# The first expert slot's rows gathered into the query load buffers, and the third value chunk joined to the first two in every second unit

## The chip, the cores and the metric

One core of a Trainium2 chip runs the program. The metric is device time in microseconds (us) of one execution. A measurement of this kernel can tell about 0.2% (2 us) from no change.

## The reference, cut to what matters

Attention comes first: 8 batches, 12 heads, 448 tokens, head size 64, with a root-mean-square norm on queries and keys. Its result is the input of a mixture of 8 experts, where each token goes to the one expert with the largest gate value.

```python
q_n, k_n = rmsnorm(q, g_q), rmsnorm(k, g_k)
scores = scale * q_n @ k_n.T
attn = exp(scores - max(scores)); attn /= sum(attn)
x = (attn @ v)                          # 3584 tokens x 768
logits = x @ w_gate + modality_bias[modality_id]
e_idx = argmax(logits)                  # one expert for each token
out[e_idx == e] = gate_w * relu(x @ w1[e]) @ w2[e]
```

## The kernel before

**Attention.** A unit is two heads of one batch, and there are 48 (NU). A unit takes 7 steps (NJ), one for each 128 of its 896 keys; step n belongs to unit i = n // 7 and has j = n % 7. In a step TensorE (PE) makes the scores of the unit itself, transposed (`st`, line 1019, two matmuls, four at j = 3), and scores of a unit two ahead for its maxima (`sa`, lines 986 and 991). ScalarE (ACT) takes the exponential of `st`; VectorE (DVE) takes the maximum of `sa`. Each of the two kinds has two PSUM buffers (`ps_s`, `ps_a`), so `st` waits for the exponential of the `st` two before it, and `sa` for the maximum of the `sa` two before it. Between these PE places, by the table PLAN, the transposes of queries and keys (`tr`, line 910), of maxima (`mt`), the value products (`av`), the sums and gate products (`sm`, lines 1083 and 1090) and the transposes of the result (`xt`, line 1127).

The value products of unit u run in the steps of unit u + 1. They come in four chunks: chunks 0 and 1 at j = 1, chunk 2 at j = 4, chunk 3 at j = 6 (`av` in PLAN is (1, 1, 4, 6)). A chunk 0 to 2 is two matmuls of 64 columns, one for each head, which the trace shows as four records. Chunk 3 holds the tail of one head and the head of the other; its weights are put together by `values(u)`, two copies of 64x64, at j = 2 of unit u + 1. `xt` of a unit runs six units later at j = 4, behind `av` and, in every fourth unit (i = 4m + 1), behind four gate products.

POOL (GpSimd) adds up the exponentials, norms queries and keys (`norm`, 26 steps ahead of its unit) and issues the indirect transfers (gathers and weights). SP issues all other transfers from one queue in order: among them the moves of queries and keys between partitions (line 923), which PE's `sa` and `st` read.

**Experts.** The tokens are worked through in slots of 256 tokens. For slot 0 the rows of x are gathered by two indirect transfers into `xrw` (`xgather`), written to a DRAM buffer (`xkeep`, line 557), read back in another layout (`xfetch`, line 563), transposed by DVE in three groups (`xturn`), and split into two parts by ACT and DVE; the first product (`mm1_half`, line 609) reads them. `xrw` holds normed queries and keys until the last unit has been transposed. `r1[0]` is the load buffer of the queries, of six units, and takes the first expert's weights (`wload`) afterwards.

Every engine's instructions run in the order in which they are written here, each engine with its own queue. A line number 52 or 53 is a recording helper's; there the tile names tell which instruction it is.

Of the kernel before, what the change touches and what calls it, by code (L numbers as in the profile page):

```python
# [19 lines left out]
NT, DM, DFF, NE = 3584, 768, 1024, 8  # L20
CP, NCH = 112, 4
NJ = 7
NP = H // 2
NU = B * NP
# [42 lines left out]
def kernel(  # L67
# [15 lines left out]
    V, A, G = (Deferred(e, n) for e, n in ((nc.vector, "op"), (nc.scalar, "act"), (nc.gpsimd, "dma")))  # L83
# [338 lines left out]
    r1 = [bp.tile([128, 3 * DFF], F32, name=f"r1_{i}") for i in range(2)]  # L422
    xrw = bp.tile([128, 4 * DM], F32, name="xrw")
# [12 lines left out]
    def view(t, off, p, *dims):  # L436
        n = 1
        for d in dims:
            n *= d
        a = t[:p, off : off + n]  # L440
        if len(dims) > 1:
            ax = " ".join("abcd"[: len(dims)])
            a = a.rearrange(f"p ({ax}) -> p {ax}", **dict(zip("abcd"[1:], dims[1:])))
        return a
# [27 lines left out]
    vd_b = [view(at_l, 8 * DM - 128 * (i + 1), 128, 128) for i in range(2)]  # L472
# [40 lines left out]
    def wload(s, which, halves=(0, 1), pairs=(0, 1)):  # L513
        tb, i = tb_of(s)
        for h in halves:
            if which == 0:
                G.indirect_dma_start(out=r1[h], out_offset=None, in_=w1v,
                                     in_offset=IOFF(ap=tb["wi"][:, i, h : h + 1], axis=0),
                                     bounds_check=NE * 256 - 1, oob_is_err=False)
                continue  # L520
            for c in pairs:
                G.indirect_dma_start(out=r2[h][:, 2 * DM * c : 2 * DM * (c + 1)], out_offset=None, in_=w2v,
                                     in_offset=IOFF(ap=tb["vi"][:, i, 2 * h + c : 2 * h + c + 1], axis=0),
                                     bounds_check=NE * DFF // 2 - 1, oob_is_err=False)
# [21 lines left out]
        return view(xrw, 0, 128, 8, DM // 4)  # L546

    def xs_(s):
        return view(xrw, 0 if s < 2 else 2 * DM, 128, 2, DM)

    def xgather(s, t):
        src = x_d[:NT1] if s < NS1 else x_d[:]
        G.indirect_dma_start(out=xs_(s)[:, t], out_offset=None, in_=src,
                             in_offset=IOFF(ap=entry(s, t)[:, 0:1].bitcast(I32), axis=0))

    def xkeep(s):
        SY.dma_start(xg_d[s].rearrange("(t p) d -> p t d", t=2), xs_(s))

    def xfetch(s):
        if s not in (0, 2):  # L560
            xkeep(s)
        for g in range(4):
            SY.dma_start(xv(s)[32 * g : 32 * g + 32],
                         xg_d[s][:, DM // 4 * g : DM // 4 * (g + 1)].rearrange("(b p) d -> p b d", p=32))
# [244 lines left out]
    if True:  # L809
# [8 lines left out]
        HB = {}  # L818
# [244 lines left out]

        def values(u):
            for h, r in enumerate((LO, HI)):
                A.copy(vd_b[u % 2][r, 64 * h : 64 * h + 64], HB[u // 3]["v"][r, u % 3, 3])

        def avcopy(u):
            t = T[u]
# [305 lines left out]
        def put(n, *what):  # L1375
            plan.setdefault(n, []).append(what)

        P = PLAN
        AVJ, XTJ, XTE, SMJ, LAJ, RCJ = (P[x] for x in ("av", "xt", "xte", "sm", "la", "rc"))
# [7 lines left out]
        def xt_at(u):  # L1387
            if u < NU - 8:
                return NJ * (u + 6) + XTJ
            return NJ * (NU - 2 + (u - NU + 8) // 2) + XTE[u % 2]  # L1390

        def when(what, u):
            return P["first"].get((what, u), NJ * u - P[what])

        for u in range(NU):
            for j in range(NJ):
                jj = ((0, 1, 2, 4, 5, 6, 3) if u < P["early"] else (3, 0, 1, 2, 4, 5, 6))[j]
                put(when("sa", u) + j * (P["sastep"] if u == 0 else 1), "sa", u, jj)
            put(when("mt", u), "mt", u)
            if u < NU - 1:  # L1400
                for c in range(4):
                    put(NJ * (u + 1) + (AVJ[c] if u < NU - 2 else min(AVJ[c], 6)), "av", u, c)
            put(xt_at(u), "xt", u)
            if u % 2:
                put(NJ * (u + 1) + (SMJ if u < NP * (B - 2) else P["sml"]), "sums", u - 1)
            if u % 4 == 3:
                put(NJ * (u + 2) + (LAJ if u < NP * (B - 2) else min(LAJ, 4)), "gates", u // 4)
                put(NJ * (u + 2) + (RCJ if u < NP * (B - 2) else min(RCJ, 6)), "recips", u // 4)
            put(when("tk", u), "tr", u, 1)
            put(when("tq", u), "tr", u, 0)  # L1410
            put(when("nq", u), "norm", u, 0)
            put(when("nk", u), "norm", u, 1)
            put(when("sk", u), "sq", u, 1)
            put(when("sq", u), "sq", u, 0)
            if ("rs", u) in P["first"]:
                put(when("rs", u), "rs", u // 3, P["rs0"].get(u, 0), u % 3 + 1)
            elif u > 8 and u % 3 == 2:
                put(when("rs", u), "rs", u // 3, 0, 3)
            if 5 < u < 10:
                put(when("ld", u), "load", u)  # L1420
            elif u > 9 and u % 2 == 0:
                put(when("ld", u) - 1, "load", u, 2, (0,))
                put(when("ld", u) + 1, "load", u, 2, (1,))

        for n in range(P["start"], NJ * NU):
# [63 lines left out]
            if 0 <= i < NU and j in CSJ:  # L1489
                h = CSJ.index(j)  # L1490
# [20 lines left out]
            if i > 0 and j == 2:  # L1511
                values(i - 1)
            if i == NU - 1 and j == 4:
                values(i)
# [9 lines left out]
            if n == P["gc2"]:  # L1524
                table_consts()
            for t in range(2):
                if n == NJ * (NU - 3) - 2 + t:
                    xgather(0, t)
            for h in range(2):
                if n == NJ * (NU - 3) - 1 + 6 * h:  # L1530
                    wload(0, 0, (h,))
            if n == NJ * (NU - 3) + 2:
                xkeep(0)
            if n == NJ * (NU - 3) + 5:
                xfetch(0)
            if i >= NU - 2 and j in P["s1"]:
                split1(P["s1"].index(j), i - NU + 2)
# [22 lines left out]
        u, g = NU - 1, NU // 4 - 1  # L1560
# [52 lines left out]
        for s in range(NSTAT):  # L1613
# [32 lines left out]
            for b_ in range(16):  # L1646
                t, j = divmod(b_, 8)
# [100 lines left out]
```

## Time and profile before

| | |
|---|---|
| median of 3 runs | 1034.41 us (1032.71 to 1034.77) |
| profiled execution | 1034.98 us, its span 1033.3 us |
| PE busy | 1013.8 us (98%) |
| DVE, ACT, POOL busy | 743.5, 709.0, 715.9 us |
| granted clock | 0.998 of full speed |

The profile is of one execution; the span runs from its first to its last instruction, and 1.7 us lie outside. Shares of busy time are averages over the attention (to about 535 us) and the experts behind it.

### The profile page before, as it was taken

To read this page: it belongs to the slowest core of one execution; us is meant where nothing else is said; L and a number is where in the kernel's file an instruction comes from. 1 tells how busy PE (TensorE), PEld (TensorE's weight loads), DVE (VectorE), ACT (ScalarE), POOL (GpSimd) and SP (SyncE) were. 2 spreads that over 40 slices of the span, in tenths; PEclk is the share of its full clock that TensorE was granted. 3 is DMA by queue.
4 is the path that set the end of the run, shared out by engine and by line. 5 is a ranking of instruction groups with operands and counts; after the bars stand their busy time and mean duration, and the time that the engine had idled before them with its cause. 6 is when DMAs were issued, how large, how long until landed. Compare 5 with 4: busy or idle time off the path is not lost. (4 is left out here: it accounts for less than half of the span.)

```text
span 1033.3 us, 18863 instructions
## 1 busy us (share of the span) xinstructions
PE 1013.8 (98%) x6462; PEld 818.9 (79%) x6462; DVE 743.5 (72%) x1260; ACT 709.0 (69%) x1379; POOL 715.9 (69%) x747
## 2 busy tenths in 40 slices
PE   9899999999999999999989999999999999999997
PEld 7655666666666666656559999999999999999995
DVE  6777888887888788886667986755685567556740
ACT  7897999889999899888655555545554455545531
POOL 7788798989788887889856646865545554565361
PEclk9999999999999999999999999999999999999999
DMA  8776667868677786766748506144572342234162
GB/s 197 187 170 138 153 141 183 178 141 185 160 168 162 160 186 148 167 116 126 228 121 286 94 20 195 32 123 123 150 279 66 119 123 79 65 105 123 40 210 92
DMA packets 147900, 148.20 MB, mean 143 GB/s; under 512 B 72702, under 2 KB 137682, under 8 KB 147284
## 3 DMA queue, kind: packets, MB, share of 16 engines
q1 hardware_dynamic: 122398, 105.08, 43.0%
q0 software_dynamic: 25328, 41.82, 12.8%
q8 instruction: 53, 0.87, 0.4%
q14 instruction: 51, 0.42, 0.2%
q10 hardware_dynamic: 70, 0.02, 0.0%
HBM read 150.31 MB, written 33.39 MB: 178 GB/s over the span
## 5 line engine op out<-in xcount | busy, mean ns | idle before, releaser
L609 PE MATMUL ph<-xw,w1w 128*128 128x256 f32 x2016 | 246.1, 284 | 1.7 <-ACT at_w2lw L52 0.8
L609 PEld LDWEIGHTS ph<-xw,w1w 128*128 128x128 f32 x2016 | 243.9, 192 | 3.3 <-issue 1.1
L52 DVE TENSOR_REDUCE at_hlw<-sa 128x1 f32<-128x448 f32 x336 | 205.1, 619 | 26.3 <-PE sa L991 24.7
L1019 PE MATMUL st<-w1w 128*128 128x448 f32 (+1 forms) x480 | 183.5, 432 | 2.4 <-ACT at_w2lw L52 1.1
L52 POOL DMA_INDIRECT r<-in_moe_w_dram,tb_w x60 | 84.0, 1399 | 53.4 <-DVE w1w L52 38.1
L52 ACT ACTIVATE hhw<-ph 128x512 fp32r<-128x512 f32 x56 | 33.5, 597 | 121.2 <-PE ph L609 121.2
L639 PE MATMUL py<-w2lw,hhw 128*128 128x384 f32 x448 | 113.8, 335 | 0.0
L52 ACT ACTIVATE r2w<-st 128x448 f32<-128x448 f32 x168 | 91.0, 544 | 32.8 <-PE st L1019 26.6
L52 DVE TENSOR_TENSOR w1w<-r,w1w 128x768 fp32r<-128x768 f32 x112 | 103.9, 958 | 11.0 <-ACT w1w L52 9.9
L991 PE MATMUL sa<-w1w 128*128 128x448 f32 (+1 forms) x288 | 108.0, 375 | 3.6 <-DVE at_hlw L52 3.3
L52 POOL DMA_INDIRECT r2w<-in_moe_w_dram,tb_vi x48 | 50.0, 1041 | 84.7 <-DVE w2lw L52 75.7
L52 ACT CAST w1w<-xw 64x448 fp32r<-64x448 f32 x188 | 105.8, 563 | 3.7 <-issue 1.4
L52 DVE TENSOR_TENSOR w2lw<-r2w,w2ha 128x1536 fp32r<-128x1536 f32 x28 | 49.1, 1757 | 81.0 <-ACT w2ha L52 81.0
L1019 PEld LDWEIGHTS st<-w1w 128*128 128x128 f32 (+1 forms) x480 | 86.1, 190 | 25.5 <-issue 10.7
L1019 PE MATMUL st<-w1w,w2ha 65*128 65x448 f32 x288 | 100.5, 369 | 0.0
L52 POOL TENSOR_TENSOR r2w<-r2w 128x448 f32<-128x448 f32 (+1 forms) x72 | 82.9, 1152 | 24.0 <-DVE r2w L52 15.1
L52 ACT ACTIVATE at_w2lw<-st 128x448 f32<-128x448 f32 x168 | 90.6, 544 | 12.1 <-PE st L1019 6.9
L52 POOL TENSOR_TENSOR xrw<-r,at_hlw 112x512 f32<-112x512 f32 x95 | 97.6, 1047 | 0.5
L52 ACT CAST w1w<-r 128x768 fp32r<-128x768 f32 x112 | 95.3, 904 | 0.1
L52 ACT ACTIVATE yw<-py,ltn 128x384 f32<-128x384 f32 x55 | 29.3, 578 | 79.1 <-PE py L639 75.5
L639 PEld LDWEIGHTS py<-w2lw,hhw 128*128 128x128 f32 x448 | 80.9, 188 | 0.0
L52 POOL TENSOR_TENSOR r2w<-r2w,at_w2lw 64x448 f32<-64x448 f32 (+1 forms) x48 | 54.7, 1140 | 31.3 <-DVE r2w L52 15.7
(302 smaller groups left out, 2208.1 us busy)
## 6 DMA issues: line engine op xcount, KB each, us to landing
w1w<-xw SPq DMA_DIRECT2D x216, 112.0 KB
xg<-xrw SPq DMA_DIRECT2D x14, 768.0 KB
xrw<-xg SPq DMA_DIRECT2D x56, 192.0 KB
r<-in_q_dram SPq DMA_DIRECT2D x19, 448.0 KB
r<-in_k_dram SPq DMA_DIRECT2D x19, 448.0 KB
w2ha<-xw SPq DMA_DIRECT2D x72, 112.0 KB
w1w<-w1w SPq DMA_DIRECT2D x48, 112.0 KB
r2w<-in_v_dram SPq DMA_DIRECT2D x24, 224.0 KB
```

The source lines that it names most:

```text
L52: return fn(*a, **kw)
L609: PE.matmul(ps[:, i], lhsT=lt_, rhs=rt_[:, c], start=n == 0, stop=n == 17)
L639: PE.matmul(ps[n][:, :384], lhsT=lt_[:, j, 128 * t : 128 * t + 128], rhs=rt_[:, 384 * n : 384 * n + 384], start=j == 0 and m == 0, stop=j ...
L991: PE.matmul(ps[:, :S], lhsT=t["qq"][r, h, a : a + 128], rhs=t["kk"][h][r], start=True, stop=True)
L1019: PE.matmul(ps[:, :S], lhsT=l, rhs=t["qq"][:, h] if first else t["ql"][0:65, h], start=first and (j != 3 or h == 0), stop=not first and (j ...
```

## The change

Three things are changed. The third chunk (c = 2) of units u = 8, 10, ..., 40 (17 units) moves from j = 4 to j = 1, behind the first two. `values` of units 8 to 41 copies on DVE instead of ACT. The rows of slot 0 are gathered into `r1[0]` (its first three query buffers, whose last reader is `norm` of unit 44) at steps 300 and 301 instead of into `xrw` at 313 and 314; `xkeep(0)` goes from step 317 to 307 and `xfetch(0)` from 320 to 312. `xfetch` still writes `xrw`.

```diff
     def xs_(s):
-        return view(xrw, 0 if s < 2 else 2 * DM, 128, 2, DM)
+        return view(r1[0], 0, 128, 2, DM) if s == 0 else view(xrw, 0 if s < 2 else 2 * DM, 128, 2, DM)
...
         def values(u):
             for h, r in enumerate((LO, HI)):
-                A.copy(vd_b[u % 2][r, 64 * h : 64 * h + 64], HB[u // 3]["v"][r, u % 3, 3])
+                copy = V.tensor_copy if 8 <= u < 42 else A.copy
+                copy(vd_b[u % 2][r, 64 * h : 64 * h + 64], HB[u // 3]["v"][r, u % 3, 3])
...
                 for c in range(4):
-                    put(NJ * (u + 1) + (AVJ[c] if u < NU - 2 else min(AVJ[c], 6)), "av", u, c)
+                    aj = AVJ[1] if c == 2 and u % 2 == 0 and 8 <= u < 41 else AVJ[c]
+                    put(NJ * (u + 1) + (aj if u < NU - 2 else min(aj, 6)), "av", u, c)
...
-                if n == NJ * (NU - 3) - 2 + t:
+                if n == 300 + 1 * t:
                     xgather(0, t)
...
-            if n == NJ * (NU - 3) + 2:
+            if n == 307:
                 xkeep(0)
-            if n == NJ * (NU - 3) + 5:
+            if n == 312:
                 xfetch(0)
```

On PE, in unit 11 (where chunks of unit 10 run), the rows before are these; `sa_4` is the `sa` of step 4.

```order
L991 MATMUL sa_0_1817<-w1w 128x448
L1061 MATMUL av_1819<-r2w,at_w2lw 64x448 x4
L1002 MATMUL mt_1824<-idn,at_hlw 7x128
...
L991 MATMUL sa_4_1868<-w1w 128x448
L1061 MATMUL av_1819<-r2w,at_w2lw 64x448 x2
L1127 MATMUL xt_1872<-idn,at_hhw 112x128 x4
L1019 MATMUL st_5_1896<-w1w 128x448 x2
```

In the changed program the same place reads as follows.

```order
L991 MATMUL sa_0_1817<-w1w 128x448
L1061 MATMUL av_1819<-r2w,at_w2lw 64x448 x6
L1002 MATMUL mt_1826<-idn,at_hlw 7x128
...
L991 MATMUL sa_4_1870<-w1w 128x448
L1128 MATMUL xt_1872<-idn,at_hhw 112x128 x4
L1019 MATMUL st_5_1896<-w1w 128x448 x2
```

Two matmuls have moved from behind `sa_4` to the four behind `sa_0`, and `xt` now follows `sa_4` at once. On DVE the two copies stand between two maxima in the changed program, ahead of the subtraction `w1w<-tr,xw`:

```order
L52 TENSOR_REDUCE at_hlw<-sa_1_1839 128x1
L52 COPY at_w2lw<-at_w2lw 64x64 x2
L52 TENSOR_REDUCE at_hlw<-sa_2_1857 128x1
L52 TENSOR_TENSOR w1w<-tr_0_1859,xw 128x448
L52 TENSOR_REDUCE at_hlw<-sa_4_1870 128x1
```

Before, the same rows stood there without the line of the copies, which ACT had. On POOL, around step 300, the changed program has the two gathers ahead of the last `norm` (the two rows `xrw<-r`, of unit 47):

```order
L379 DMA ltn<-l_d,ta_lr 128x4
L52 DMA r_0_158<-x_d,ltn 128x768
L52 TENSOR_TENSOR r2w<-r2w 128x448
L52 TENSOR_TENSOR at_hhw<-r2w 128x448
L52 DMA r_0_158<-x_d,ltn 128x768
L52 TENSOR_TENSOR xrw<-r_0_158,at_hlw 112x2x4x64
L52 TENSOR_TENSOR xrw<-r_1_159,at_hlw 112x2x4x64
```

Before, both gathers stood ten rows further on, behind the norms and eight additions, right ahead of the first weights' transfer.

## Rows read from the trace of the kernel before

**Rows 1.** Busy time by stage: stretch, length, then each engine's busy time.

```profile
94.00:422.00 328.00, 328.00 (x1807) 208.21 (x1807) 271.82 (x530) 293.82 (x685) 276.62 (x317) 1.00 0.73 164
520.00:537.00 17.00, 14.19 (x80) 9.23 (x74) 13.45 (x18) 10.22 (x22) 7.64 (x9) 1.00 0.44 94
```

**Rows 2.** Timeline of PE in unit 27: start, length, instruction, count.

```profile
314.25 1.72 PE L1061 MATMUL av<-r2w 128*64 128x448 f32 x8
315.91 0.28 PE L1002 MATMUL mt<-idn,at_hlw 128*7 128x128 f32 x1
...
318.49 0.37 PE L991 MATMUL sa<-w1w 128*128 128x448 f32 x1
318.79 0.97 PE L1061 MATMUL av<-r2w 128*64 128x448 f32 x4
319.69 0.65 PE L1127 MATMUL xt<-idn,at_hhw 128*112 128x128 f32 x4
320.09 0.65 PE L1019 MATMUL st<-w1w 128*128 128x448 f32 x2
```

**Rows 3.** Timeline of PE in unit 46, an `xt` without value products ahead.

```profile
516.44 0.37 PE L1019 MATMUL st<-w1w,w2ha 65*128 65x448 f32 x1
516.65 0.60 PE L1127 MATMUL xt<-idn,at_hhw 128*112 128x128 f32 x4
517.00 0.64 PE L1019 MATMUL st<-w1w 128*128 128x448 f32 x2
```

**Rows 4.** Timeline of DVE and PE, end of unit 27 and start of 28.

```profile
317.87 0.62 DVE L52 TENSOR_REDUCE at_hlw<-sa 128x1 f32<-128x448 f32 x1 [0.40 <-PE sa L991]
...
318.82 0.62 DVE L52 TENSOR_TENSOR w1w<-tr,xw 128x448 fp32r<-128x448 f32 x1 [0.33 <-ACT xw L52]
...
321.60 0.61 DVE L52 TENSOR_REDUCE at_hlw<-sa 128x1 f32<-128x448 f32 x1
...
322.56 0.37 PE L986 MATMUL sa<-xw 128*128 128x448 f32 x1
```

**Rows 5.** Busy time of DVE alone, from that subtraction to that maximum's end.

```profile
318.82:322.21 3.39, 3.25 (x11) 1.00 0.75 173
```

**Rows 6.** DVE's groups of instructions from 100 to 420 us: total, mean ns.

```profile
L52 DVE SCALAR_TENSOR_TENSOR r2w<-r2w,half 128x448 f32<-128x448 f32 x16 | 12.3, 770 | 0.0
...
L52 DVE TENSOR_TENSOR at_hlw<-sp,rs 112x64 f32<-112x64 f32 x14 | 2.3, 218 | 0.2
...
L52 DVE TENSOR_TENSOR ra<-lo,ra 112x32 f32<-112x32 f32 x5 | 1.0, 196 | 0.2
```

**Rows 7.** Timeline of ACT in unit 27, the exponentials of its last two steps.

```profile
320.84 1.16 ACT L52 ACTIVATE at_w2lw<-st 128x448 f32<-128x448 f32 x2 [0.15 <-PE st L1019]
```

**Rows 8.** Timeline of the end of the attention, slot 0's rows being turned.

```profile
511.30 0.38 SPq L557 DMA_DIRECT2D xg<-xrw  x1
...
526.75 1.15 DVE L52 STREAM_TRANSPOSE r2w<-xrw 128x512 f32<-128x512 f32 x1 [2.75 <-DMA xrw<-xg]
...
527.93 0.62 ACT L52 CAST xw<-r2w 128x512 fp32r<-128x512 f32 x1 [1.36 <-DVE r2w L52]
...
530.56 0.62 ACT L52 CAST xw<-r2w 128x512 fp32r<-128x512 f32 x1 [0.61 <-DVE r2w L52]
...
529.57 0.68 PE L1019 MATMUL st<-w1w 128*128 128x448 f32 x2 [1.07 <-ACT at_w2lw L52]
```

**Rows 9.** Timeline of POOL and PE, the last norm and the gathers.

```profile
488.95 2.04 POOL L52 TENSOR_TENSOR xrw<-r,at_hlw 112x512 f32<-112x512 f32 x2
...
502.87 0.94 POOL L52 DMA_INDIRECT xrw<-x_d,ltn  x1 [0.30 <-issue]
...
493.08 0.55 PE L910 MATMUL tr<-idn,xrw 112*128 112x112 f32 x4
```

**Rows 10.** Timeline of POOL and DVE beside each other, units 26 and 27.

```profile
312.52 1.54 DVE L52 SCALAR_TENSOR_TENSOR r2w<-r2w,half 128x448 f32<-128x448 f32 x1
...
316.51 2.05 POOL L52 TENSOR_TENSOR xrw<-r,at_hlw 112x512 f32<-112x512 f32 x2
```

## Prediction

> **What bounds the kernel now.** I read the busy time by stage first. From 94 to 422 us, the body of the attention, PE is busy for all of 328.00 us, and ACT, POOL and DVE for 294, 277 and 272 [rows 1]. So in this stage whatever PE no longer has to do shortens the kernel, but only until another engine's chain becomes the later one: ACT has a tenth of the stage free, and a stall of PE can come from a local chain long before an average is full. Then I read the stretch where attention ends: of 17 us PE is busy for 14.19 [rows 1], the largest hole behind the start. The timeline of that stretch says why: DVE waits 2.75 us for the rows of slot 0 to come back from DRAM, ACT waits for DVE, and PE waits 1.07 us for ACT (three shorter waits follow) [rows 8]. Those two places are what the change touches.
>
> **The third chunk, as PE sees it.** In unit 27 the run of two chunks takes from 314.25 to 315.91, 1.66 us, and the lone chunk from 318.79 to 319.69, 0.90 us [rows 2]. A third chunk inside the run therefore costs 1.66 - 0.90 = 0.76 us. The lone chunk starts 0.30 us behind `sa`, and from `xt` behind it to the next `st` are 0.40 us: 0.30 + 0.90 + 0.40 = 1.60 us from `sa` to `st` [rows 2]. Where no value product stands ahead, `xt` starts 0.21 us behind the matmul before it and `st` 0.35 us later, 0.56 us [rows 3]. So step 4 loses 1.04 us, step 1 gains 0.76, and PE's own saving is 0.28 us. This holds for the 8 of the 17 units where `xt` follows at once (u = 10, 14, ..., 38). In the other nine (u = 8, 12, ..., 40) gate products stand between; no row shows them right behind `sa`. They start between 0.21 and 0.30 us behind it, so the saving is 0.90 - 0.76 = 0.14 at the least and 0.23 at the most. Gate products are matmuls of few columns like the value chunk, which starts after 0.30, so I take 0.14. Sum on PE alone: 8 x 0.28 + 9 x 0.14 = 3.5 us.
>
> **What the other engines let through.** Up to `sa` of step 4 ACT and DVE follow PE as before; then PE asks for their work 1.04 us sooner. In unit 27 DVE's chain from the subtraction at 318.82, which waits for ACT and so for `tr` on PE, to the maximum that ends at 321.60 + 0.61 = 322.21 is busy for 3.25 of 3.39 us: it can't move up [rows 4, 5]. The first `sa` of unit 28, at 322.56, needs that maximum's PSUM buffer. It can come 322.56 - 322.21 = 0.35 us sooner, less 0.05 for the hand-over (an estimate): 0.30 instead of 1.04. The chain is this long because six small instructions of the routing stand in it. Such a routing occurs five times from 100 to 420 us [rows 6], and by the program's order all five stand in step 4 of one of the 8 units (11, 15, 23, 27, 35). There 0.74 us are given back, 5 x 0.74 = 3.7 us. The three others have no routing; on ACT the exponential of step 5 had been idle for 0.15 us only [rows 7], but the next product needs it only behind chunk 3, and ACT also loses the two copies. I take no loss there; the bound is 3 x 0.74 = 2.2 us. In the nine units with gate products 0.90 us are asked for, and the gate products and `xt` still lie between, so no loss. Attention in all: 3.5 - 3.7, or 0.2 us slower, bounded by 3.5 faster and, with the three, 2.4 slower.
>
> **The copies.** ACT is relieved of 34 pairs. In unit 27 its exponentials wait for PE's `st` anyway, so I count nothing; the bound is in the term above. On DVE no copy of this form is in the trace. The nearest row by size is a product of 112x64 at 0.22 us [rows 6]: 0.45 for two. They land where DVE idles 0.40 us ahead of the next maximum and 0.33 ahead of the subtraction [rows 4], 0.73 in all, so they are covered. If they take longer than that, all of the rest goes into the chain above.
>
> **Slot 0.** Gathers 13 steps sooner, the store 10 and the fetch 8 steps (a step is some 1.36 us: `sa` of step 4 of unit 27 at 318.49, of step 7 at 322.56 [rows 2, 4]) bring the fetch to before 515 us, well ahead of DVE's first turn at 524.0 (526.75 less the wait). The wait of 2.75 us goes. What is late next is ACT: the first group's cast moves up by its own wait of 1.36 us only, since the exponential ahead of it is PE's pace; of the second cast's 0.61 I take half, as DVE's turns now wait for ACT's casts between them [rows 8]. 1.36 + 0.30 = 1.65 us for PE; bounds 0 (if the weights' casts alone hold PE) and 2.8 (17.00 - 14.19 [rows 1]).
>
> **What the gathers are put in front of.** On POOL a gather takes 0.94 us with 0.30 of issue ahead of it, 1.24 us [rows 9], and two now stand ahead of unit 47's norm, which ended at 488.95 + 2.04 = 490.99 us. It would end at 490.99 + 2.48 = 493.47, and the transposes that read it start at 493.08: up to 0.39 us of stall, down to 0 if POOL's idle time takes them. I take 0.35. Further on POOL is even, since the gathers are gone there. The weights of slot 0 now wait on POOL for the store to have read `r1[0]`; the store ends some 500 us by the same shift, before they are due.
>
> **The sum.** - 0.2 + 1.65 - 0.35 = 1.1 us faster. The profiled execution took 1034.98 us (span 1033.3 and 1.7 around it): it would take 1033.9. It lies 0.57 us above the median, 1034.41, for which I predict **1033.3 us**.
>
> **Rivals.**
> (a) DVE's chain gives way and all of PE's saving comes through: 3.5 + 1.65 - 0.35 = 4.8, 1029.6 us; with the whole wait at the end 1028.5. For it: PE's side is certain to 0.1 us, and 8 + 9 units repeat it. Against it: rows 4 and 5 show no gap in that chain.
> (b) Slower: the copies on DVE are held up by POOL. At 317.5 us, where they go in, POOL is in the middle of two norms of 1.02 us each, and a DVE instruction that met a POOL addition took 1.54 us against a mean of 0.77 in its group [rows 6, 10]. If each pair waits for one norm, it is 1.02 + 0.45 = 1.47 us long, 0.74 over the cover; in the five units that is 3.7 us, 1037.0. If both copies wait, 2.49 - 0.73 = 1.76, times five 8.8, 1042.1. It decides from 0.73 + 1.1 / 5, about 0.95 us for a pair. The Trainium skill speaks for this: its page SBUF — State Buffer (Who interferes with whom) says that a VectorE copy in a two-port mode and a GpSimd instruction exclude each other, the later one fully blocked. The row with 1.54 us agrees for an instruction with two inputs; no row shows it for a copy.
> (c) SP stands still. It issues in order, and the store of slot 0 now stands ahead of unit 47's moves. The second gather was issued at 502.87 and the store went out at 511.30, 8.4 us later [rows 8, 9]. Issued near 490, the gather would then hold SP to 498.7 and six moves behind it at some 0.6 us each would come at up to 502.5, for an `sa` near 504: up to 2 us, 1035.3. Against it: weights were being loaded at 504 us, and not at 490, so the gather should land in about half the time.
> That the change doesn't do what it says can be left out: the order shows both moves.
>
> **Chances.** Forecast 0.42, its own range 1031.8 to 1035.0; (a) 0.28; (b) 0.20; (c) 0.10. Faster by over 0.2% means under 1032.3: (a) and 0.08 of the forecast, 0.36. Slower means over 1036.5: 0.17 of (b) and 0.01 of the forecast, 0.18. Within: 0.33 + 0.03 + 0.10 = 0.46. The range goes from 1029.5 (the middle of (a); 0.11 is left out below) to 1037.2 (one norm; 0.08 is left out above).
>
> **What would show it.** In the new trace of units 11, 15, 23, 27, 35 PE should wait for DVE's maximum at the first `sa` of the next unit, and those pairs of units should be some 0.45 us longer; units with gate products should be 0.14 shorter. The DVE copies' length against 0.95 us decides on (b). At the end DVE's wait for the fetch should be gone and PE's holes there should come to about 1.2 us instead of 2.8. At 493 us `tr` should wait under 0.5 us for the norm. I am wrong if PE waits in units 9 to 42 come to more than 4.5 us or to less than 1.5, or if a new wait stands at unit 47.

## The result, and the profile after

The changed kernel takes 1047.09 us (median of 4 runs, 1046.81 to 1050.16) where the kernel before takes 1033.99: a ratio of 1.0133, with a 95% interval of 1.0121 to 1.0146. That is 13 us slower, where 1.1 us faster was forecast, and outside the range. The profiled execution has a span of 1045.3 us, 12.0 more than before.

Busy time by stage of the changed kernel, as [rows 1] has it for the kernel before; the end of the attention now lies 13 us later:

```profile
94.00:422.00 328.00, 319.65 (x1742) 201.89 (x1742) 299.53 (x562) 272.91 (x610) 267.84 (x305) 0.99 0.70 157
533.00:550.00 17.00, 15.27 (x86) 9.65 (x80) 14.05 (x21) 10.02 (x22) 10.14 (x10) 1.00 0.15 45
```

In the body of the attention PE, busy throughout before, has lost 8.4 us to idleness, and DVE's busy time has risen from 271.82 to 299.53. The end has improved: 15.27 of 17 us are busy instead of 14.19. So the loss is in the body, and DVE got more work there than the two short copies per unit should bring. DVE's groups of instructions from 100 to 420 us (total in us, mean in ns) say what it is:

```profile
L52 DVE TENSOR_REDUCE at_hlw<-xrw 112x8 f32<-112x512 f32 x60 | 40.5, 675 | 0.0
L52 DVE COPY at_w2lw<-at_w2lw 64x64 f32<-64x64 f32 x28 | 24.3, 869 | 0.2
L52 DVE COPY at_w2lw<-r2w 64x64 f32<-64x64 f32 x26 | 20.2, 775 | 0.2
```

A copy of 64 elements a partition takes 0.8 us in the mean, longer than a reduction of 512. The timeline of unit 26 shows why: DVE, POOL and PE where the copies for unit 25 stand (`values` runs one unit later).

```profile
310.66 3.74 DVE L52 COPY at_w2lw<-r2w 64x64 f32<-64x64 f32 x2
314.43 0.19 DVE L52 TENSOR_SCALAR rs<-sp 112x32 f32<-112x32 f32 x1
...
315.04 0.62 DVE L52 TENSOR_TENSOR lg<-sp,rs 112x64 f32<-112x64 f32 x4
...
310.03 0.96 POOL L1235 DMA_INDIRECT l_d<-ltk,posi  x1 [0.16 <-issue]
311.01 2.05 POOL L52 TENSOR_TENSOR xrw<-r,at_hlw 112x512 f32<-112x512 f32 x2
313.01 1.13 POOL L52 TENSOR_TENSOR r2w<-r2w 128x448 f32<-128x448 f32 x1
314.30 0.96 POOL L1235 DMA_INDIRECT l_d<-ltk,posi  x1 [0.17 <-issue]
...
315.81 0.88 PE L1128 MATMUL xt<-idn,at_hhw 128*112 128x128 f32 x4 [2.17 <-DVE lg L52]
```

The pair starts while POOL issues an indirect transfer, and then POOL works through three instructions that stand one behind the other, to 313.01 + 1.13 = 314.14. The first copy takes 3.54 us and ends 0.06 us behind the last of them; the second takes 0.19 us. Behind the copies DVE's small products on `sp` are late, and PE waits 2.17 us for them at `xt`. Elsewhere the same pair can be short; these rows are of units 14 (the pair starts 0.06 us into an indirect transfer of POOL) and 40 (POOL idle to 466.18):

```profile
180.47 0.38 DVE L52 COPY at_w2lw<-r2w 64x64 f32<-64x64 f32 x2
...
180.41 0.96 POOL L1235 DMA_INDIRECT l_d<-ltk,posi  x1 [0.15 <-issue]
...
465.48 0.38 DVE L52 COPY at_w2lw<-at_w2lw 64x64 f32<-64x64 f32 x2
...
466.18 0.27 POOL L53 TENSOR_TENSOR at_hlw<-at_hlw 112x48 f32<-112x48 f32 x1 [1.36 <-ACT at_hlw L53]
```

What PE waited for from 100 to 480 us (sum, times, longest):

```profile
PE sa L991 <- DVE at_hlw L52: 3.5, 10, 0.8
PE sa L986 <- DVE at_hlw L52: 3.0, 6, 0.6
PE xt L1128 <- DVE lg L52: 2.2, 1, 2.2
PE xt L1128 <- DVE at_hlw L52: 0.8, 2, 0.4
PE st L1019 <- ACT r2w L52: 0.6, 1, 0.6
```

All but 0.6 of these 10.1 us are waits for DVE. In the kernel before, PE waited in the same stretch for 0.9 us (0.5 for ACT, 0.4 for DVE).

### The profile page after: what moved, and what is told of

It is laid out like the page before. It is cut to its first block, busy times and chain, and to the rows that moved or that the text cites. A ratio compares the mean times of both kernels' runs of the same rounds, so it can differ in the third digit from the quotient of the medians.

```text
span 1045.3 us, 18868 instructions
## 1 busy us (share of the span) xinstructions
PE 1017.9 (97%) x6462; PEld 819.4 (78%) x6462; DVE 791.2 (76%) x1328; ACT 693.1 (66%) x1311; POOL 711.2 (68%) x747
## 5 line engine op out<-in xcount | busy, mean ns | idle before, releaser
L991 PE MATMUL sa<-w1w 128*128 128x448 f32 (+1 forms) x288 | 110.5, 384 | 7.1 <-DVE at_hlw L52 6.4
```

The source lines that it names most:

```text
L991: PE.matmul(ps[:, :S], lhsT=t["qq"][r, h, a : a + 128], rhs=t["kk"][h][r], start=True, stop=True)
```

## The experiments

Eleven kernels undo, isolate or rewrite parts, and one cuts the copies. To say where a difference lies, each profiled execution is cut at instructions that all programs share. Of PE's eight `st` of 65x448 in a unit, the profile names eight `st<-w1w,w2ha` in three units of four and none in the fourth, six in the mean; number 6u + 1 of these is called mark u here. It is the same instruction in every program, but only every fourth mark (8, 12, ..., 44) is the start of the unit of its number: mark 9 lies in unit 8, mark 42 in unit 41, mark 47 in unit 46. B is from mark 9 to mark 42, C on to mark 47, D from there to the end of the span, which the profile gives to 0.1 us. B, C and D are each of one execution: e2's was the fastest of its five and e11's the slowest of its seven. The part ahead of B differed by up to 2.1 us between executions, with the kernel before the longest; no edit touches it. Each ratio is against runs of the kernel before on the same chip.

| kernel | ratio (95%) | B, us | C, us | D, us |
|---|---|---|---|---|
| before | 1 | 344.35 | 50.32 | 516.86 |
| changed | 1.0133 (1.0121 to 1.0146) | 358.02 | 51.66 | 515.98 |
| e1 chunk alone | 1.0035 (1.0022 to 1.0049) | 347.95 | 50.35 | 516.73 |
| e2 copies on DVE alone | 1.0174 (1.0151 to 1.0196) | 359.99 | 51.75 | 517.01 |
| e3 slot 0 alone | 1.0003 (0.9991 to 1.0015) | 345.59 | 53.05 | 516.17 |
| e4 changed, copies as maxima | 1.0215 (1.0199 to 1.0231) | 368.74 | 51.37 | 516.00 |
| e5 changed, copies on ACT | 1.0032 (1.0013 to 1.0051) | 346.91 | 52.15 | 516.85 |
| e6 changed, copies as reductions | 1.0027 (1.0012 to 1.0041) | 347.28 | 52.98 | 516.74 |
| e7 reductions alone | 1.0018 (1.0004 to 1.0032) | 346.66 | 51.53 | 517.97 |
| e8 chunk in gate units alone | 0.9991 (0.9974 to 1.0009) | 343.98 | 50.23 | 518.41 |
| e9 as e8, and slot 0 behind the norm | 1.0007 (0.9996 to 1.0018) | 343.78 | 51.79 | 515.77 |
| e10 slot 0 behind the norm alone | 1.0011 (0.9997 to 1.0025) | 344.29 | 53.04 | 516.65 |
| e11 chunk in the other eight units | 1.0044 (1.0027 to 1.0061) | 352.85 | 50.30 | 516.58 |
| e12 changed, copies halved | 1.0279 (1.0258 to 1.0301) | 373.25 | 51.49 | 515.76 |

**e1, the chunk alone.** The kernel before with this:

```diff
-put(NJ * (u + 1) + (AVJ[c] if u < NU - 2 else min(AVJ[c], 6)), "av", u, c)
+aj = AVJ[1] if c == 2 and u % 2 == 0 and 8 <= u < 41 else AVJ[c]
+put(NJ * (u + 1) + (aj if u < NU - 2 else min(aj, 6)), "av", u, c)
```

> The kernel before with the third chunk's move alone; the copies of `values` stay on ACT. Theory L (the copies on DVE wait for POOL's instructions, and that is the loss): 1032 to 1036 us; the nine units with gate products give back some 0.17 us each (pairs of units in the changed kernel whose copies ran in 0.19 us), the others between 0.2 of gain and 0.45 of loss. Theory M (the moved chunk is the loss, since DVE's chain is then late at the next unit): 1042 us or more, with PE waiting for a maximum at the first `sa` of units 12, 16, 24, 28 and 36.

1.0035, some 3.6 us: that is 1037.6 us on the scale of the expectation, over theory L's range (up to 1036) and well short of theory M (from 1042). PE, DVE and PE again at the end of unit 27, as in [rows 2] and [rows 4]:

```profile
315.21 2.48 PE L1061 MATMUL av<-r2w 128*64 128x448 f32 x12
317.61 0.28 PE L1002 MATMUL mt<-idn,at_hlw 128*7 128x128 f32 x1
...
320.17 0.36 PE L991 MATMUL sa<-w1w 128*128 128x448 f32 x1
320.37 0.60 PE L1127 MATMUL xt<-idn,at_hhw 128*112 128x128 f32 x4
320.73 0.65 PE L1019 MATMUL st<-w1w 128*128 128x448 f32 x2
...
320.51 0.62 DVE L52 TENSOR_TENSOR w1w<-tr,xw 128x448 fp32r<-128x448 f32 x1 [0.33 <-ACT xw L52]
...
323.30 1.15 DVE L52 TENSOR_REDUCE at_hlw<-sa 128x1 f32<-128x448 f32 x2
...
323.00 0.47 PE L1019 MATMUL st<-w1w 128*128 128x448 f32 x1
323.31 0.36 PE L1019 MATMUL st<-w1w,w2ha 65*128 65x448 f32 x1
323.96 0.47 PE L986 MATMUL sa<-xw 128*128 128x448 f32 x1 [0.29 <-DVE at_hlw L52]
```

The run with the third chunk takes 317.61 - 315.21 = 2.40 us instead of 1.66, and from `sa` to `st` of step 4 PE now needs 0.56 us instead of 1.60, as worked out. But DVE's chain from the subtraction to the last maximum starts 320.51 - 320.17 = 0.34 us behind that `sa`, as before (0.33), and is as long as before (2.79 to the start of the maximum, 2.78 before), so the next unit's `sa` waits. From mark 11 to mark 13, a stretch with one moved chunk (in unit 11), it is 162.60 - 136.47 = 26.13 us here and 163.36 - 137.78 = 25.58 before: 0.55 longer.

**e2, the copies alone.** The kernel before with this:

```diff
-A.copy(vd_b[u % 2][r, 64 * h : 64 * h + 64], HB[u // 3]["v"][r, u % 3, 3])
+copy = V.tensor_copy if 8 <= u < 42 else A.copy
+copy(vd_b[u % 2][r, 64 * h : 64 * h + 64], HB[u // 3]["v"][r, u % 3, 3])
```

> The kernel before with the copies of `values` on DVE alone. Theory L: 1043 to 1048 us, the copies take 0.19 us where POOL is idle and else end some 0.05 us behind a POOL instruction, mean about 0.8. Theory M: 1034 to 1036.

1.0174, over theory L's range: the copies alone are slower than the whole change. They take 0.88 us in the mean:

```profile
L52 DVE COPY at_w2lw<-at_w2lw 64x64 f32<-64x64 f32 x36 | 30.7, 852 | 0.3
L52 DVE COPY at_w2lw<-r2w 64x64 f32<-64x64 f32 x32 | 28.9, 903 | 0.2
```

A stall like that of unit 26 comes twice here: PE waits 2.17 us at `xt` in unit 14 and 1.97 in unit 26, and these units are 3.8 and 3.7 us longer than before. In the changed kernel the pair of unit 14 took only 0.38 us (the row at 180.47). So what the copies cost depends on what POOL is doing when they come, and that is not the same in two programs.

**e3, slot 0 alone.** The last three pieces of the diff and the first (`xs_`), nothing of the chunk and the copies.

> The kernel before with the early gathers, store and fetch of slot 0 alone. Both theories: 1032 to 1034 us, some 0.9 us under before, as the changed kernel gained from its unit 47 to its end; DVE's wait of 2.75 us for the rows is gone.

1.0003: no change, where 0.9 us were expected. The end (D) is 0.7 us shorter, but C is 2.73 longer. 1.28 of that lies in unit 42, and e2 and e7, in which slot 0 is as before, are longer there by 1.48 and 1.25; 1.44 lies in unit 44, with the wait of `tr` behind the gathers. POOL and PE around unit 47's norm, as in [rows 9]:

```profile
488.64 0.95 POOL L52 DMA_INDIRECT r<-x_d,ltn  x1 [0.30 <-issue]
489.60 1.16 POOL L52 TENSOR_TENSOR r2w<-r2w 128x448 f32<-128x448 f32 x1
...
492.12 0.96 POOL L52 DMA_INDIRECT r<-x_d,ltn  x1
493.11 2.04 POOL L52 TENSOR_TENSOR xrw<-r,at_hlw 112x512 f32<-112x512 f32 x2
...
495.20 0.60 PE L910 MATMUL tr<-idn,xrw 112*128 112x112 f32 x4 [1.22 <-POOL xrw L52]
```

The wait comes again in e5 and e6 (1.24 and 1.26 us), which have the same early gathers, and in none of e1, e2, e7, e8 and e11, which do not.

**e4, a maximum instead of the copy.** The changed kernel; the result of each instruction is the same block.

```diff
-copy(dst, src)
+V.tensor_tensor(out=dst, in0=src, in1=src, op=ALU.max)
```

> The changed kernel, with each copy of 64x64 on DVE written as the maximum of the block and itself, a two-input instruction with the same result. Theory L: the two-input form does not wait for POOL; each takes 0.2 to 0.4 us, and the kernel 1032 to 1036. Rival to L (any DVE instruction at that place waits, because of the place and not of the copy's form): these take 0.8 us in the mean again and the kernel 1044 to 1048.

1.0215: the two-input form waits as the copy does, and longer, so the refinement in theory L that it would not is refuted:

```profile
L52 DVE TENSOR_TENSOR at_w2lw<-at_w2lw 64x64 f32<-64x64 f32 x36 | 38.7, 1075 | 0.3
L52 DVE TENSOR_TENSOR at_w2lw<-r2w 64x64 f32<-64x64 f32 x32 | 25.9, 810 | 0.2
```

Either every instruction at this place waits, or the forms that wait are more than copies. The next two kernels tell these apart.

**e5, the copies back on ACT.** The changed kernel with `A.copy` for all units.

> The changed kernel with the copies of `values` back on ACT, so the moved chunk and slot 0 together. Theory L (all loss beyond these two is the copies' wait for POOL): 1.002 to 1.005 of before, the sum of the chunk alone (1.0035) and slot 0 alone (1.0003). Rival S (the moved chunk leaves DVE and ACT so little room that part of the loss stays): 1.008 or more.

1.0032, as theory L has it: B falls from 358.02 to 346.91, so in the changed kernel the copies cost 11.1 us of B. The rest, 2.6 us, came with the chunk.

**e6, a reduction instead of the copy.** The changed kernel, with copies on DVE, at the same place, of the same block:

```diff
-copy(dst, src)
+V.tensor_reduce(out=dst, in_=src.unsqueeze(2), axis=AX.X, op=ALU.max)
```

> The changed kernel, with each copy of 64x64 on DVE written as a maximum over an axis of one element, a reduction with one input and the same result. Theory L2 (an instruction of DVE with two inputs from SBUF waits for POOL as a copy does, a reduction does not; in the trace of before the reductions of 112x512 took 0.66 to 0.69 us with POOL busy or idle): 0.17 to 0.3 us each, the kernel 1.002 to 1.005 of before. Rival P (the place makes any DVE instruction wait): 0.8 us or more in the mean, 1.013 or more.

1.0027, as with the copies on ACT: theory L2 holds and rival P is refuted. No reduction took over 0.22 us, with POOL busy or idle:

```profile
L52 DVE TENSOR_REDUCE at_w2lw<-at_w2lw 64x64 f32<-64x64 f32 x36 | 7.5, 209 | 0.3
L52 DVE TENSOR_REDUCE at_w2lw<-r2w 64x64 f32<-64x64 f32 x32 | 6.7, 209 | 0.2
```

So it is the form of the instruction, not its place. What the copies wait for can be read from their ends: 43 of the 68 copies of the changed kernel took over 0.25 us, and all 43 end 0.045 to 0.06 us behind the end of an instruction of POOL. The Trainium skill states this split on its page SBUF — State Buffer (Who interferes with whom): a VectorE copy in a two-port mode shuts GpSimd out and the other way round, an instruction with two SBUF inputs contends with a GpSimd one that reads SBUF, and a `tensor_reduce` never contends on trn2. The traces agree: the copies wait (0.88 us in the mean in e2), the instructions with two SBUF inputs wait (0.95 in e4), the reductions do not (0.21 in e6). No run shows in which mode the copies ran.

**e7, the reductions alone.** The kernel before with e6's edit.

> The kernel before with these reductions on DVE in place of the copies on ACT, nothing else changed. Theory L2: 0.999 to 1.002 of before, since they are covered by DVE's idle time of 0.73 us. Rival P: 1.017 as with the copies alone.

1.0018, interval 1.0004 to 1.0032: at the upper end of what theory L2 gave, and clearly not rival P. Relieving ACT of the copies gains nothing even where the copies wait for nobody.

**e8, the chunk in the nine units with gate products.** As e1 with `u % 4 == 0` in place of `u % 2 == 0`.

> The kernel before with the third chunk moved only in the nine units with gate products behind it (u = 8, 12, ..., 40), none of which stands ahead of a unit with a routing. If PE's own saving comes through there, 0.14 to 0.21 us each: 1.3 to 1.9 us, 0.998 to 0.999 of before. If the two units in which the run with the chunk alone waited for a DMA by 0.9 us (21 and 33) wait again: 0.9995 to 1.0005.

0.9991, interval 0.9974 to 1.0009. The saving can't be told from none by the times, but the trace shows it: from mark 9 to mark 11 (the moved chunk of unit 9) it takes 135.99 - 120.19 = 15.80 us instead of 137.78 - 121.77 = 16.01, and from mark 13 to 15 it takes 16.23 instead of 16.38. B as a whole is only 0.4 us shorter, since units 19, 20 and 39 came out 0.75 us longer in this execution. PE waits for no DMA from 225 to 440 us.

**e9 and e10, the gathers behind the norm.** In e10 slot 0 is early as in e3, but with these steps; e9 adds e8's edit.

```diff
-if n == 300 + 1 * t:
+if n == 304 + 1 * t:
...
-if n == 307:
+if n == 310:
...
-if n == 312:
+if n == 315:
```

> The kernel before with slot 0 early and both gathers behind unit 47's norm, nothing else. Theory N (in the run of slot 0 alone the gain of about 1.1 us at the end was eaten by the 1.22 us that `tr` waited for the norm behind the gathers): that wait is gone, the holes at the end stay at about 1.7 us, 0.9985 to 0.9995 of before. Rival (the end gains nothing that can be measured): 1.000.

> The kernel before with the third chunk moved in the nine units with gate products alone, and slot 0 early, but with both gathers behind unit 47's norm on POOL (steps 304 and 305, store at 310, fetch at 315). If both parts keep what they gain: 1.3 us from the chunk and 1.1 us at the end, some 0.998 of before. If POOL is as late for the next transposes as it was for `tr` with the gathers ahead of the norm: 0.9985 to 1.000.

1.0011 and 1.0007: no gain, as e10's rival has it, and neither of the expectations that gave one came true. In e10 the wait of `tr` is gone, since the gathers now follow the norm, but C stays at 53.04 us. Unit 42 is 1.23 us longer than before, with a wait of `sm` for POOL that e2 and e7 have too, with no gather near; and units 44 and 45 are 0.63 and 0.89 longer. One row of PE in unit 45:

```profile
504.56 0.44 PE L991 MATMUL sa<-w1w 128*128 128x448 f32 x1 [0.67 <-DMA w1w<-xw]
```

It is for one of the moves, behind the store and the gathers in time; in e9 the same wait is 0.41. e9's profiled span, 1031.5 us, is the shortest of all, but its median is not below that of before.

**e11, the chunk in the other eight units.** As e1 with `u % 4 == 2`.

> The kernel before with the third chunk moved in the eight units without gate products alone (u = 10, 14, ..., 38), five of which have a routing. Theory R (the routing units pay 0.55 us each, the three others nothing): 2.75 us, 1.0025 to 1.003 of before, and with the 0.9991 of the other nine nearly the 1.0035 of all 17. Rival D (the two waits for a DMA in units 21 and 33 come with the move and make up part of it): they come here too, 1.004 or more.

1.0044 (1.0027 to 1.0061): rival D's side, though theory R's 1.003 is in the interval. In its trace, of an execution 2.9 us over the median, PE waits twice for a move in unit 21, and B is 352.85. But waits of this kind stand in traces without the chunk too (e3 and e7, below), so rival D isn't shown.

```profile
250.78 0.47 PE L1019 MATMUL st<-w1w,w2ha 65*128 65x448 f32 x1 [1.02 <-DMA w1w<-xw]
...
253.10 0.71 PE L991 MATMUL sa<-w1w 128*128 128x448 f32 x1 [0.84 <-DMA w1w<-xw]
```

**e12, the copies halved.** The changed kernel, each copy cut into two of 64x32.

```diff
-copy(dst, src)
+for m in range(2):
+    V.tensor_copy(dst[:, 32 * m : 32 * m + 32], src[:, 32 * m : 32 * m + 32])
```

> The changed kernel, with each copy of 64x64 on DVE cut into two of 64x32. In the traces so far, instructions of DVE of up to 32 elements a partition with two inputs from SBUF took 0.17 to 0.20 us while POOL was busy (over 100 of them), those of 64 and more waited. Theory Z (the size decides: a small one does not wait for POOL): 0.15 to 0.2 us for each of the 136, the kernel 1.002 to 1.005 of before. Rival F (the form decides, and those small ones did not wait for another reason): the mean of one is 0.4 us or more, some single ones over 1 us, the kernel 1.012 or more.

1.0279, the slowest of all: rival F. Smaller copies wait too, up to 3.53 us: 48 of the 136 took over 0.25 us, against 43 of 68 in the changed kernel, and together they keep DVE for 69.8 us instead of 55.4:

```profile
L52 DVE COPY at_w2lw<-at_w2lw 64x32 f32<-64x32 f32 x72 | 42.3, 629 | 0.3
L52 DVE COPY at_w2lw<-r2w 64x32 f32<-64x32 f32 x64 | 27.5, 472 | 0.2
```

The expectation's reason for theory Z was a misreading: the small instructions of the routing that it counted (`ra<-lo,ra` and its like, 112x32) do not have two inputs from SBUF. `ra` is a PSUM tile (line 1166 of the kernel before), so like the product on `sp` they read one input from SBUF and one from PSUM. They say nothing on size.

## Why the prediction was wrong, step by step

**The copies: the step that failed.** The prediction took "a product of 112x64 at 0.22 us: 0.45 for two", covered by DVE's idle 0.73, because no copy of this form was in the trace. That product reads one input from PSUM (`sp`), and with POOL busy or not it takes the same 0.22; a copy within SBUF is not its equal, and the row was the nearest by size but not by operands. Measured: 0.18 to 0.19 us when POOL is idle, and else mostly up to the end of an instruction of POOL, a mean of 0.82 for the 54 copies of 100 to 420 us ((24.3 + 20.2) / 54), 1.65 for a pair, well over the 0.95 from which the prediction let (b) decide. The price is 11.1 us (changed against e5), and PE's 10.1 us of waits are over the 4.5 that the prediction named as a sign of being wrong. This was rival (b), with a chance of 0.20. Its mechanism is the right one, shown by e2, e4 and e6; its price, 3.7 to 8.8 us, fell short for three reasons. It reckoned with one norm for a pair or one for each copy; a copy can wait through three POOL instructions (3.54 us in unit 26). It let only the five units with a routing pay; but unit 26, which has none, alone became 3.9 us longer, and the copies delay the maxima in other units too, where `sa` at line 991 waits, ten times. And a stall costs more than its length: behind the 2.17 us in unit 26 the granted clock, by stretches of the changed kernel, is this:

```profile
313.50:315.80 2.30, 0.14 (x4) 0.02 (x1) 2.19 (x9) 0.17 (x2) 2.11 (x3) 1.00 0.24 55
315.80:318.50 2.70, 2.69 (x10) 2.38 (x11) 2.70 (x5) 0.54 (x1) 1.76 (x2) 0.54 0.19 43
318.50:321.00 2.50, 2.50 (x12) 1.79 (x11) 2.50 (x6) 2.14 (x5) 0.53 (x1) 0.81 0.40 112
```

The third number from the end of a row is the granted clock. After 2.3 us with PE nearly idle it is 0.54 and then 0.81: first almost all at 1.2 GHz, then back to 2.4. That loses 0.46 x 2.70 + 0.19 x 2.50 = 1.7 us more (an estimate from these rows), and from mark 27 to mark 28 it is 20.96 us instead of 17.07, 3.9 more: 2.17 + 1.7.

**The chunk on PE.** Right: 0.74 us more in step 1 (0.76 forecast), 1.04 less in step 4. In units with gate products 0.21 and 0.15 us are gained (e8), where 0.14 was taken, with 0.23 as the other bound.

**What the other engines let through.** The mechanism is right: in the five units with a routing DVE's chain doesn't move, and the next unit's first `sa` waits (in e1 in units 12, 16, 24, 28 and 36, 0.27 to 0.29 us); a stretch with one of them is 0.55 us longer (0.46 forecast). What was taken too lightly are the three units without a routing: the units 19 and 31 gained nothing in e5 and e11 (each 0.09 longer instead of 0.28 shorter), 39 was 0.5 shorter there, but 0.1 longer in e6. And there is a cost that no term had: `st` or `sa` waited for a move between partitions. From 225 to 440 us these waits of PE come to 1.1 us in e1, 0.6 in e5, 1.1 in e6 and 2.3 in e11, which have the chunk in the eight units; but also to 0.6 in e3 and 1.0 in e7, which don't, and to nothing in the changed kernel and e12, and 0.3 in e4, which do. Whether the chunk makes such a wait likelier, and why the moves come late, stays open. In all, the chunk alone came out at 3.6 us slower by the times and by B, against 0.2 slower in the forecast and a bound of 2.4.

**Slot 0.** DVE's wait of 2.75 us is gone, as said: in the changed kernel its first turn starts without a wait. That turn, the third one and PE's holes at the end are these:

```profile
536.81 1.13 DVE L52 STREAM_TRANSPOSE r2w<-xrw 128x512 f32<-128x512 f32 x1
...
545.17 1.11 DVE L52 STREAM_TRANSPOSE r2w<-xrw 128x512 f32<-128x512 f32 x1
...
544.29 1.69 PE L609 MATMUL ph<-xw,w1w 128*128 128x256 f32 x12 [0.39 <-ACT at_w2lw L52]
546.98 0.39 PE L609 MATMUL ph<-xw,w1w 128*128 128x256 f32 x1 [1.00 <-ACT xw L52]
547.71 0.86 PE L609 MATMUL ph<-xw,w1w 128*128 128x256 f32 x5 [0.34 <-DVE xw L52]
```

The holes come to 1.73 us instead of 2.80, so 1.07 us are gained where 1.65 were taken: what was late next was ACT's cast of the last group, which waits 1.65 us for DVE's third turn. The other half of the sum, the norm behind the gathers, was mis-sized because it rested on one trace: in that of before the norm ended 2.09 us ahead of `tr`, but in e1, e2, e7 and e8 1.06 or 1.07 us ahead, without any gather in front (and 2.41 in e11). So `tr` waited 1.22 us in e3, where at most 0.39 was allowed. In the changed kernel, already late for other reasons, `tr` waits for nothing there. Nor does it help to move the gathers (e10). On the whole slot 0 is worth nothing that can be measured.

**Rival (c)** did not show as told: PE waited for no move in units 44 to 47 of the changed kernel or of e3. Its argument against itself held: from the second gather to the store it took 4.3 us in e3 and 5.1 in the changed kernel, against 8.4 before. The 0.67 us in e10 and 0.41 in e9, where a move came late behind the store, may be a small form of it; that was not tested.

**The adding up.** B of the changed kernel is 13.67 us longer than before: 11.1 for the copies, 2.6 with the chunk (e5 against before; waits for a move are in it). C adds 1.3 (in it lie 1.4 us for which `sa` waits for DVE in unit 41, behind the last long copy), D gives back 0.9, and the part ahead of B was 2.1 shorter in this execution than in that of before: 12.0, the difference of the spans.

## What to carry to other kernels

Before work is moved to VectorE beside a busy GpSimd, look at its operands, not at its size: a copy within SBUF, or an instruction with two SBUF inputs, may wait for up to three of GpSimd's instructions, while a reduction over an axis of one element copies the same block in 0.21 us and waits for nobody. A moved chunk of TensorE's work gains only where no other engine's chain ends right behind it, so it pays unit by unit (here, by the traces, nine of seventeen, and too little for the times to show), and slack that is read from one trace (2.09 us for the norm) can be half of that in the next kernel.

## What the hardware did that was not expected

A VectorE copy could wait for more than the one GpSimd instruction that it met. Of the 43 copies of the changed kernel that took over 0.25 us, 24 ended behind the first GpSimd instruction to end after their start, 15 behind the second and 4 behind the third or fourth (indirect transfers not counted). A gap between GpSimd's instructions is not needed for a copy to get through: in 19 of the 43 cases the trace shows none before the next one. These rows of unit 36 have both, DVE's pair and then POOL:

```profile
420.74 2.47 DVE L52 COPY at_w2lw<-at_w2lw 64x64 f32<-64x64 f32 x2
...
420.01 1.14 POOL L52 TENSOR_TENSOR at_w2hb<-r2w,at_w2lw 128x448 f32<-128x448 f32 x1
421.11 2.04 POOL L52 TENSOR_TENSOR xrw<-r,at_hlw 112x512 f32<-112x512 f32 x2
423.12 1.14 POOL L52 TENSOR_TENSOR r2w<-r2w 128x448 f32<-128x448 f32 x1
```

The first copy takes 0.46 us and ends behind the first of POOL's four instructions, the second takes 1.99 and ends behind the third; POOL goes on without a gap each time. What decides when a copy gets its turn stays open. One pattern stands out: in the changed kernel, e2, e4 and e12 eight copies (or maxima) started up to 0.25 us into an indirect transfer of GpSimd and took 0.17 to 0.21 us, while all ten that started 0.63 to 0.67 us into one waited through the next three instructions, 3.49 to 3.56 us. Why was not tested.

Two-input instructions waited longer in the mean than copies in the same place (0.95 us over e4's 68, (38.7 + 25.9) / 68, against 0.81 for the copies of the changed kernel). The routing's `ra<-lo,ra`, of 112x32, with one input from SBUF and one from PSUM, took 0.20 us every time in all fourteen traces, 62 times of them with POOL in the middle of a norm or an addition.
